# Moving the linear part of a fused attention and MLP kernel to another fill of its group

## The chip, the cores and the metric

The kernel runs on one core of one Trainium2 chip. The metric is device time of one execution in microseconds (us), as the median over several executions. Engines: PE is TensorE (matmuls), PEld its weight loads, DVE is VectorE, ACT is ScalarE, POOL is GpSimd, SP is SyncE.

## The reference

```python
# x: (4, 12480, 128), inducing: (32, 128), w_in: (128, 2048), w_out: (2048, 128)
def mab(q, kv):                      # softmax attention, scale 1/sqrt(128)
    s = scale * (q @ kv.transpose(0, 2, 1))
    a = softmax(s)
    return a @ kv
h = mab(I, x)                        # 32 inducing points read x
y = mab(x, h).reshape(-1, 128)       # each token reads the 32 points
z = y @ w_in
out = (max(z, 0) + alpha * min(z, 0)) @ w_out
```

The kernel never forms y. With e the unnormalised softmax of a token and hW = h @ w_in, it computes relu(e @ hW) @ ((1 - alpha) * w_out), plus a linear part e @ hA with hA = h @ (w_in @ (alpha * w_out)), and divides by the softmax sum at the end.

## The kernel before

Tokens are worked in groups of 512: 24 groups per batch, and one of 192 tokens (the remainder). A full group takes four *fills*, j = 0 to 3. A fill's four ring matmuls write one *ring bank* each, of six PSUM buffers used in turn; an *eviction* reads a bank with ReLU, and the bank is free for the next matmul when it ends. A *hold* here is time in which PE waits with its next matmul for another engine. The unit of time below is the *slot*: everything that PE executes from one fill's first matmul to that of the next.

```python
    def fill(st, g, j):
        ...
        for r in range(4):
            ps = bank()                       # next of the 6 PSUM ring banks
            for i in range(cp):
                mm(ps[:, i * t : (i + 1) * t],
                   st.hW[32 * r : 32 * r + 32, j * cp + i, :],
                   rep[32 * r : 32 * r + 32, :t])
            banks.append(ps)
        lin = j == 2 // cp and lin_groups(st.b, g)      # third fill
        if lin:
            linear(st, lin)
        bits, pos = plan[st.b * NG + g, j]
        for r, ps in enumerate(banks):
            if r == pos:
                flush()                       # finish of the group before
            if bits >> r & 1:                 # evict with ReLU on ACT ...
                pin(nc.scalar.activation(out=gt[:, r, :w], in_=ps[:, :w], func=RELU))
            else:                             # ... or on DVE
                pin(nc.vector.tensor_relu(gt[:, r, :w], ps[:, :w]))
        flush()
        return gt

    def lin_groups(b, g):                     # for even g: this group and the next
        if g % 2 == 0 and (b, g) != (0, 0):
            return [g, g + 1] if g + 1 < NS * NQ else [g]
        return []

    def linear(st, groups):                   # 8 small matmuls, two row groups side by side
        for k in range(NB):
            for r, g in enumerate(groups):
                ...
                    mm(accs[(st.b * NG + g) % 2][:pp, k, :],
                       st.rep[g][32 * r : 32 * r + 32, k * pp : (k + 1) * pp],
                       st.hA[32 * r : 32 * r + 32, :],
                       start=((r == 1 or cp > 1) and k == 0), stop=False, ...)

    def finish(st, g):                        # L446: DVE reads the accumulator, divides
        ...
        pin(nc.vector.tensor_tensor(out=ob[...], in0=acc[...], in1=rbc, op=MULT))
        ...                                   # L451: DMA of ob to out

    for b, g, j in fills:                     # the main loop
        gt = fill(states[b], g, j)
        for fn, _ in tasks.pop((b * NG + g, j), []):
            fn()                              # misc tasks of this slot
        if prev is not None:
            mm2(*prev)                        # 16 matmuls of the fill before, into acc
        prev = (states[b], g, j, gt)
```

There are two accumulators: even groups use one, odd groups the other. The linear part of an even group g also starts the accumulator of group g + 1, which is the one that group g - 1 used. That group's `finish` stands in fill (g, 1).

The misc tasks prepare the next batch and the next 2048 tokens: `a_scores` (first fill of odd groups), `a_accum` (accumulation over x, third fill of even groups), `b_scores` or `b_den` (last fill of even groups, in turn; `b_den` makes softmax denominators; `h_den`, once for each next batch, those of h, beside `b_scores`). Each takes a ring bank. `make_plan` is a search in the kernel that decides, from a cost model of the slots, which evictions go to ACT (`bits`) and where the finish stands (`pos`).

The softmax here doesn't subtract the row's maximum and nothing guards it: scores larger than these inputs give would overflow.

## Time and profile before

| | before |
|---|---|
| time, first measured | 617.91 us |
| a plain fill, start to start | 1.327 us |
| slot with the linear part alone, held / free | 1.840 / 1.543 us |
| eviction of 128x512 | ACT 0.60, DVE 0.69 us |
| finish of a full group (ob) on DVE | 0.68 us |

The page's first lines (engine: busy us, share of the span, instructions):

```profile
span 615.7 us, 21682 instructions
## 1 busy us (share of the span) xinstructions
PE 596.0 (97%) x9179; PEld 436.4 (71%) x9180; DVE 520.3 (84%) x899; ACT 507.6 (82%) x998; POOL 89.0 (14%) x151
```

PE sets the pace, but 97% doesn't say that it never stands still. The Trainium skill ("Perfetto Trace Analysis", section "Tensor Engine Instruction (MATMUL, LD_WEIGHTS)") says that the profiler computes a matmul's end from its size and a delay for SBUF. The trace agrees that the spans are no measure of throughput: the 16 matmuls of a fill into its accumulator use the whole array and start 0.056 us apart, yet each is drawn 0.22 us long. So starts are what to read.

The timeline of DVE and PE around the third fill of an even group (start us, length us, engine, line, operation, out<-in, shape, count):

```profile
273.65 0.69 DVE L397 TENSOR_SCALAR gt<-ring_85 128x512 bf16<-128x512 f32 x1
...
274.25 0.68 DVE L446 TENSOR_TENSOR ob<-acc_87,rd 128x512 f32<-128x512 f32 x1
274.46 0.38 PE L94 MATMUL ring_82<-rep,hW 32*128 32x512 bf16 x1
...
274.68 0.21 PE L94 MATMUL acc_88<-hA,rep 32*128 32x128 bf16 x1
...
274.99 0.21 PE L94 MATMUL acc_87<-hA,rep 32*128 32x128 bf16 x1
274.99 0.22 PE L94 MATMUL acc_88<-hA,rep 32*128 32x128 bf16 x1
275.04 0.21 PE L94 MATMUL acc_87<-hA,rep 32*128 32x128 bf16 x1
```

The linear part starts at 274.68 in the even accumulator, acc_88. Its second matmul, into acc_87, starts 0.31 us later. Between them nothing happens on PE but the end of modelled spans. The finish of the odd group before, which reads acc_87, ends at 274.25 + 0.68 = 274.93; the semaphore that ended the matmul's wait was updated at 274.95. This is hold 1.

The timeline of PE and ACT a little earlier, around the last fill of an even group and the first of the odd group:

```profile
240.37 0.39 PE L94 MATMUL ring_84<-rep,hW 32*128 32x512 bf16 x1
...
240.70 0.25 PE L94 MATMUL ring_82<-pick,e_4543 128*128 128x4 bf16 x4
240.81 1.05 PE L94 MATMUL acc_88<-W_169,gt 128*128 128x128 bf16 x16
...
241.34 0.59 ACT L395 ACTIVATE gt<-ring_85 128x512 bf16<-128x512 f32 x1
241.80 0.38 PE L94 MATMUL ring_83<-rep,hW 32*128 32x512 bf16 x1
241.80 0.39 PE L94 MATMUL ring_84<-rep,hW 32*128 32x512 bf16 x1
241.98 0.37 PE L94 MATMUL ring_85<-rep,hW 32*128 32x512 bf16 x1
241.99 0.38 PE L94 MATMUL ring_86<-rep,hW 32*128 32x512 bf16 x1
```

This last slot, with b_den, takes 241.80 - 240.37 = 1.43 us. In the odd group's first fill the third ring matmul starts 0.18 us after the second: it needs ring_85, which the second ACT eviction of the fill before gave free at 241.93. This is hold 2.

### The profile page before, as it was taken

Reading aid. Unit: us, or ns where it says so; the run is one execution under the profiler, and the core shown is the slowest. Engines: PE = TensorE matmul, PEld = TensorE weight load, DVE = VectorE, ACT = ScalarE, POOL = GpSimd, SP = SyncE. Lnnn points to the kernel's source line nnn. Section 1 sums busy time; section 2 is a strip of 40 time slices with the busy share of each in tenths; the row PEclk is TensorE's granted clock in tenths of the full one; section 3 lists DMA queues with packets and bytes.
Section 4 is the critical chain, followed back from the end, with each engine's and each line's share of the span. In section 5 each row is a group of like instructions: output and inputs, shape, how many; then the busy total and the mean of one; then the engine's idle time right before and its main releaser. Section 6 shows DMA issues by size and latency. Waiting matters only on the chain. (4 is left out here: it accounts for less than half of the span.)

```text
span 615.7 us, 21682 instructions
## 1 busy us (share of the span) xinstructions
PE 596.0 (97%) x9179; PEld 436.4 (71%) x9180; DVE 520.3 (84%) x899; ACT 507.6 (82%) x998; POOL 89.0 (14%) x151
## 2 busy tenths in 40 slices
PE   5899999999999999999999999999999999999995
PEld 4577776777777777777777777777777777777774
DVE  4588888888888888888989898888888888888884
ACT  3688888888888888888888888888888888888884
POOL 7142112010011111110111111100101110110010
PEclk9999999999999999999999999999999999999998
DMA  9824999742125689972123599986112231221211
GB/s 142 172 69 93 185 168 169 155 115 69 65 85 129 137 151 175 155 160 88 56 80 94 112 185 164 162 154 138 53 60 76 87 96 46 87 96 45 88 56 43
DMA packets 87457, 68.66 MB, mean 111 GB/s; under 512 B 53200, under 2 KB 80736, under 8 KB 87360
## 3 DMA queue, kind: packets, MB, share of 16 engines
q0 software_dynamic: 21456, 39.82, 27.7%
q1 hardware_dynamic: 65904, 27.45, 23.5%
q8 instruction: 72, 1.18, 0.9%
q14 instruction: 25, 0.20, 0.1%
HBM read 39.94 MB, written 28.62 MB: 111 GB/s over the span
## 5 line engine op out<-in xcount | busy, mean ns | idle before, releaser
L94 PEld LDWEIGHTS <-gt 128*128 128x128 bf16 x6272 | 352.5, 98 | 73.6 <-issue 67.7
L94 PE MATMUL acc_87<-W_169,gt 128*128 128x128 bf16 (+1 forms) x3136 | 208.9, 220 | 0.0
L94 PE MATMUL acc_88<-W_169,gt 128*128 128x128 bf16 (+1 forms) x3136 | 208.8, 220 | 0.0
L451 POOL DMA_DIRECT2D out_dram<-ob x99 | 53.6, 541 | 501.8 <-DVE ob L446 445.0
L395 ACT ACTIVATE gt<-ring_84 128x512 bf16<-128x512 f32 (+1 forms) x162 | 96.9, 598 | 18.2 <-ACT gt L395 14.6
L395 ACT ACTIVATE gt<-ring_82 128x512 bf16<-128x512 f32 (+1 forms) x159 | 95.4, 600 | 14.8 <-ACT gt L395 9.7
L94 PE MATMUL ring_83<-rep,hW 32*128 32x512 bf16 (+1 forms) x269 | 101.1, 379 | 0.0
L94 PE MATMUL ring_84<-rep,hW 32*128 32x512 bf16 (+1 forms) x270 | 101.1, 378 | 0.0
L94 PE MATMUL ring_86<-rep,hW 32*128 32x512 bf16 (+1 forms) x267 | 100.4, 379 | 0.0
L94 PE MATMUL ring_81<-rep,hW 32*128 32x512 bf16 (+1 forms) x265 | 99.6, 379 | 0.7 <-ACT gt L395 0.4
L395 ACT ACTIVATE gt<-ring_86 128x512 bf16<-128x512 f32 (+1 forms) x149 | 89.2, 599 | 13.3 <-ACT gt L395 8.8
L94 PE MATMUL ring_85<-rep,hW 32*128 32x512 bf16 (+1 forms) x266 | 99.5, 378 | 0.0
L94 PE MATMUL ring_82<-rep,hW 32*128 32x512 bf16 (+1 forms) x263 | 98.8, 379 | 0.0
L395 ACT ACTIVATE gt<-ring_81 128x512 bf16<-128x512 f32 (+1 forms) x143 | 85.7, 599 | 15.5 <-ACT gt L395 11.6
L395 ACT ACTIVATE gt<-ring_85 128x512 bf16<-128x512 f32 x147 | 88.2, 600 | 11.4 <-ACT gt L395 7.8
L395 ACT ACTIVATE gt<-ring_83 128x512 bf16<-128x512 f32 (+1 forms) x142 | 84.9, 598 | 11.6 <-ACT gt L395 6.5
L397 DVE TENSOR_SCALAR gt<-ring_83 128x512 bf16<-128x512 f32 (+1 forms) x122 | 83.5, 685 | 12.0 <-PE ring_84 L94 5.6
L397 DVE TENSOR_SCALAR gt<-ring_81 128x512 bf16<-128x512 f32 (+1 forms) x117 | 80.1, 685 | 12.4 <-PE ring_83 L94 3.8
L397 DVE TENSOR_SCALAR gt<-ring_86 128x512 bf16<-128x512 f32 x113 | 77.6, 687 | 13.3 <-PE ring_81 L94 8.2
L397 DVE TENSOR_SCALAR gt<-ring_85 128x512 bf16<-128x512 f32 (+1 forms) x113 | 77.1, 683 | 11.2 <-PE ring_81 L94 4.4
L397 DVE TENSOR_SCALAR gt<-ring_84 128x512 bf16<-128x512 f32 x102 | 70.1, 688 | 12.1 <-PE ring_85 L94 6.2
L397 DVE TENSOR_SCALAR gt<-ring_82 128x512 bf16<-128x512 f32 x99 | 68.0, 687 | 11.2 <-PE ring_83 L94 5.6
(330 smaller groups left out, 388.1 us busy)
## 6 DMA issues: line engine op xcount, KB each, us to landing
out_dram<-ob POOLq DMA_DIRECT2D x96, 256.0 KB, 2.7
rep<-e2d SPq DMA_DIRECT2D x92, 128.0 KB, 3.4
xn<-in_x_dram POOLq DMA_DIRECT2D x18, 512.0 KB, 6.3
xn<-in_x_dram POOLq DMA_DIRECT2D x12, 256.0 KB, 7.2
w_out_f<-in_moe_w_out_dram POOLq DMA_DIRECT2D x1, 1024.0 KB, 14.2
w_in_b<-in_moe_w_in_dram POOLq DMA_DIRECT2D x1, 512.0 KB, 12.2
xT<-xn SPq DMA_TRANSPOSE x18, 6.6
out_dram<-ob POOLq DMA_DIRECT2D x3, 96.0 KB, 2.0
```

The source lines that it names most:

```text
L94: return pin(nc.tensor.matmul(o, lhsT, rhs, start=start, stop=stop, **kw))
L395: pin(nc.scalar.activation(out=gt[:, r, :w], in_=ps[:, :w], func=RELU))
L397: pin(nc.vector.tensor_relu(gt[:, r, :w], ps[:, :w]))
L451: pin((nc.sync if last_one else nc.gpsimd).dma_start(out=out[t0 : t0 + pp * nb, :].rearrange("(p j) c -> p j c", j=nb), in_=ob[:pp, :nb, :],))
```

## The change

Its intent is to put the linear part into the last fill of the even group instead of the third, and to move the accumulation over x along with it. This is the whole diff; the search for the eviction plan runs anew on the moved costs.

```diff
-        lin = j == 2 // cp and lin_groups(st.b, g)
+        lin = j == NJ // cp - 1 and lin_groups(st.b, g)
...
-                at(k + 8, lambda n=n, u=u: a_accum(states[n], u), 2, (240, "D", 220))
+                at(k + 8, lambda n=n, u=u: a_accum(states[n], u), 3, (240, "D", 220))
...
-            lin = 240 if j == 2 // cp and lin_groups(b, g) else 0
+            lin = 240 if j == NJ // cp - 1 and lin_groups(b, g) else 0
```

## The prediction

> **What bounds the kernel now.** TensorE. On the page PE is busy 97% of 615.7 us, at a granted clock of 0.996; ACT 82% and DVE 84% evict PSUM with slack. In the timeline of PE a plain fill (4 ring matmuls, then 16 into an accumulator) repeats every 1.327 us; odd groups, finish included, run at that pace. Small holds hide in the 97%, because the modelled matmul spans overlap, so I read start-to-start times in the timeline.
>
> They show two holds.
> 1. The linear part. Its first matmul (even group's accumulator) starts 0.226 us after the fill's first. The second (odd group's accumulator) starts 0.30 us later in about 40 of 48 slots, 0.004 us later in the others: 0.05 us after the VectorE finish (ob, L446) of the previous odd group has ended reading that accumulator. That finish takes 0.68 us and stands behind an eviction. Held slots last 1.840 us, free ones 1.543 us (linear alone: 0.217 us). Later matmuls wait too: the Trainium skill, "TensorE: Matmul & The Clock Gate", Part 2, says that matmuls stay in program order and only weight loads are pulled ahead; the trace agrees, all later matmuls start after the held one. Sum: 12.0 us. The view of waits doesn't list it, as each gap between modelled spans is small.
> 2. Odd groups' first fills, after a short last slot of an even group (1.43 us, with the softmax denominators, b_den): third and fourth ring matmul wait 0.175 us for evictions. Sum: 5.4 us.
>
> **What the change does.** PE executes the same instructions. The linear part moves from the even group's third to its last fill, 1.33 us later; the accumulation over x (a_accum, 0.338 us of PE) moves along, so it still shares the linear's slot, now with b_scores (0.330 us) or b_den (0.100 us). The eviction plan is searched anew.
>
> - Hold 1 goes: the finish ends 0.25 us after the old linear start, so about 1.1 us before the new. Minus 12 us, all on the critical engine.
> - Hold 2 mostly goes: the even group's last slot grows from 1.43 to 1.64 us or more, so evictions are done before the next fill. Minus 2 to 4 us.
> - New holds: the last slot takes up to 6 ring banks at once, and 7 where a_accum, b_scores and h_den meet (three times), more than the ring's 6. Estimate: plus 0.5 to 2.5 us.
>
> ACT and DVE should give nothing back: odd groups already run plain fills with a finish without holds.
>
> **Predicted:** 604.0 us, range 601.5 to 608.0. Chances: faster by over 2% 0.70; within 2% 0.29; slower by over 2% 0.01. Hold 1 alone brings about 605.8, right at the 2% mark; hold 2 decides the side.
>
> **What would show it.** Right: the second linear matmul starts within 0.01 us of the first in all even groups; slots with linear and a_accum lose 0.30 us; ring matmuls of odd groups' first fills no longer split 2 and 2; plain fills stay at 1.327 us; ACT and DVE busy times unchanged. Wrong: linear still held, or third fills of even groups longer than 1.33 us, or a_scores slots longer.
>
> **What would make it wrong.** The new plan piles evictions on one engine; the bunched bank demand stalls the PE; the evictors used the held time to catch up, so that stalls reappear in following fills. Then the time lies at 606 to 611 us, within 2%.

## The result, and the profile after

| | before | after |
|---|---|---|
| median us (6 runs each) | 617.84 | 601.05 |
| lowest to highest us | 617.36 to 618.08 | 600.25 to 601.29 |

The ratio is 0.9728, 95% interval 0.9716 to 0.9741. The result is correct. The change is clearly faster by over 2%, and the time lies 0.45 us below the predicted range. Two repeats of the same kernel beside later experiments gave medians of 602.15 and 601.80 us, inside the range; the last experiment looks at why they differ. The miss of 0.45 us is thus smaller than the 1.1 us between two medians of the same kernel.

The page after:

```profile
span 599.0 us, 21695 instructions
## 1 busy us (share of the span) xinstructions
PE 581.7 (97%) x9180; PEld 434.7 (73%) x9180; DVE 521.2 (87%) x902; ACT 507.1 (85%) x995; POOL 89.2 (15%) x151
```

DVE and ACT do the same work (521.2 and 507.1 us) in a shorter span. PE is still "97% busy".

The timeline of PE and DVE after, in the last slot of the even group and the first of the odd group, with the finish of the odd group before:

```profile
232.41 0.68 DVE L446 TENSOR_TENSOR ob<-acc_87,rd 128x512 f32<-128x512 f32 x1
...
233.94 0.38 PE L94 MATMUL ring_83<-rep,hW 32*128 32x512 bf16 x1
...
234.17 0.21 PE L94 MATMUL acc_88<-hA,rep 32*128 32x128 bf16 x1
234.17 0.21 PE L94 MATMUL acc_87<-hA,rep 32*128 32x128 bf16 x1
...
234.49 0.25 PE L94 MATMUL ring_81<-pick,e_4540 128*128 128x4 bf16 x4
234.67 0.41 PE L94 MATMUL ring_82<-xn,e1T 128*32 128x128 bf16 x16
235.01 1.07 PE L94 MATMUL acc_88<-W_169,gt 128*128 128x128 bf16 x16
235.04 0.68 DVE L397 TENSOR_SCALAR gt<-ring_86 128x512 bf16<-128x512 f32 x1
...
236.01 0.39 PE L94 MATMUL ring_83<-rep,hW 32*128 32x512 bf16 x1
236.01 0.38 PE L94 MATMUL ring_84<-rep,hW 32*128 32x512 bf16 x1
236.02 0.39 PE L94 MATMUL ring_85<-rep,hW 32*128 32x512 bf16 x1
236.02 0.38 PE L94 MATMUL ring_86<-rep,hW 32*128 32x512 bf16 x1
```

The finish ends at 233.09, the linear pair starts together 1.08 us later (234.17), and the last slot is 2.07 us long. Its last eviction ends at 235.72, and the four ring matmuls of the odd group's first fill start together (236.01 and 236.02). Hold 1 is gone in all slots; hold 2 stays in 3 of the 48 first fills of odd groups (29 before).

To see where the time went I added up, from the trace's start times, all slots of one kind (remainder groups and the first four groups of the run apart). Sums in us of the traces; an E label is an experiment below:

| slots | before | after | E1 | E3 | E5 | E6 | E8 |
|---|---|---|---|---|---|---|---|
| even groups, third | 89.58 | 61.39 | 70.33 | 77.71 | 61.09 | 63.03 | 117.55 |
| even groups, last | 71.04 | 87.70 | 80.96 | 71.02 | 91.69 | 80.14 | 70.96 |
| odd groups, first | 72.67 | 68.03 | 68.03 | 72.74 | 68.05 | 78.24 | 72.55 |
| odd groups, third | 61.58 | 61.41 | 61.40 | 65.16 | 61.59 | 61.41 | 61.41 |
| odd groups, last | 62.02 | 62.01 | 62.02 | 62.02 | 62.02 | 62.34 | 73.84 |
| everything else | 258.86 | 258.47 | 258.12 | 258.73 | 258.23 | 258.27 | 260.80 |
| span | 615.75 | 599.01 | 600.86 | 607.38 | 602.67 | 603.43 | 657.11 |

From before to after, the third and last slots of even groups lose (89.58 + 71.04) - (61.39 + 87.70) = 11.53 us. The starts of the linear matmuls show 12.0 us of hold gone there, so new costs of about 0.5 us came in. The first slots of odd groups lose 4.64 us, all else 0.57 us.

### The profile page after: what moved, and what is told of

Same layout as the page of the kernel before. It is cut to its first block, busy times and chain, and to the rows that moved or that the text cites. A ratio compares the mean times of both kernels' runs of the same rounds, so it can differ in the third digit from the quotient of the medians.

```text
span 599.0 us, 21695 instructions
## 1 busy us (share of the span) xinstructions
PE 581.7 (97%) x9180; PEld 434.7 (73%) x9180; DVE 521.2 (87%) x902; ACT 507.1 (85%) x995; POOL 89.2 (15%) x151
## 4 chain that ended last, share of the span: by engine, by line
PE 94%; DMA 2%; POOL 2%; ACT 1%; issue 0%; DVE 0%; POOLq 0%
PE acc_88 L94 33%; PE acc_87 L94 33%; PE ring_82 L94 5%; PE ring_86 L94 5%; PE ring_84 L94 5%; PE ring_81 L94 4%; PE ring_83 L94 4%; PE ring_85 L94 4%; DMA xn<-in_x_dram 2%; POOL xn L125 1%; ACT gt L395 0%; POOL xnr L130 0%; PE ring_84 L156 0%; ACT rep L327 0%; ACT e1T L185 0%
## 5 line engine op out<-in xcount | busy, mean ns | idle before, releaser
L395 ACT ACTIVATE gt<-ring_81 128x512 bf16<-128x512 f32 x144 | 86.2, 599 | 13.6 <-ACT gt L395 6.4
L395 ACT ACTIVATE gt<-ring_83 128x512 bf16<-128x512 f32 (+1 forms) x143 | 85.5, 598 | 11.9 <-PE ring_86 L94 4.3
L397 DVE TENSOR_SCALAR gt<-ring_86 128x512 bf16<-128x512 f32 x115 | 79.0, 687 | 7.2 <-PE ring_82 L94 2.5
L397 DVE TENSOR_SCALAR gt<-ring_84 128x512 bf16<-128x512 f32 x104 | 71.5, 688 | 9.4 <-PE ring_86 L94 4.4
L397 DVE TENSOR_SCALAR gt<-ring_82 128x512 bf16<-128x512 f32 x101 | 69.4, 687 | 7.4 <-PE ring_84 L94 2.5
```

## The experiments

The main theory: the second linear matmul waited for the finish of the odd group before (hold 1), and a short last slot let evictions fall behind the next fill (hold 2). The rivals: the linear pair was slow for another reason; the moved accumulation or the new eviction plan brought the gain. All twelve runs gave correct results.

### E1: the linear part alone

```diff
-        lin = j == 2 // cp and lin_groups(st.b, g)
+        lin = j == NJ // cp - 1 and lin_groups(st.b, g)
-            lin = 240 if j == 2 // cp and lin_groups(b, g) else 0
+            lin = 240 if j == NJ // cp - 1 and lin_groups(b, g) else 0
```

> The linear part alone moves to the last fill of the even group; the accumulation over x stays in the third fill. Theory (the hold on the finish goes, and the longer last slot lets evictions finish): the 12.0 us of linear holds go and most of the 5.4 us of holds in odd groups' first fills too, since the last slot grows by 0.217 us: 601 to 603 us. Rival (the bunching of tasks or the move of the accumulation is needed for the rest): only the 12 us go, 605 to 606 us.

Measured: 603.18 us, ratio 0.9769 (0.9753 to 0.9785), a little above the expected 601 to 603. Both holds are gone: the linear pair starts together, and odd groups' first slots sum to 68.03 us as in the changed kernel. So the linear part alone brings most of the gain (14.3 of 16.8 us). The even third and last slots are 2.2 us longer than in the changed kernel (151.29 against 149.09): in 26 of the third fills the fourth ring matmul is held about 0.12 us. The trace shows what precedes 24 of these: there the search has put the finish ahead of all evictions of the fill before (it starts 0.10 us into that fill, elsewhere about 1.1 us). E3 shows that this delays the evictions and so the next fill. Why the search chose it is open.

### E2: the accumulation alone

```diff
-                at(k + 8, lambda n=n, u=u: a_accum(states[n], u), 2, (240, "D", 220))
+                at(k + 8, lambda n=n, u=u: a_accum(states[n], u), 3, (240, "D", 220))
```

> The accumulation over x alone moves to the last fill; the linear part stays. Theory: the linear holds stay at about 12 us; of the holds in odd groups' first fills only those after last slots that now have b_den and an accumulation go (9 of them, 1.6 us); 615.5 to 617 us. Rival (the move of the misc tasks carries a good part of the gain): 612 us or less.

Measured: 616.73 us, ratio 0.9987 (0.9972 to 1.0002). Hold 1 stays at 12.0 us. Of the 29 held first fills of odd groups 13 are free, where 9 had been expected; 12 of them follow a last slot that got an accumulation and so grew (9 with b_den, 3 with h_den). Three others are newly held, by 0.07 us. The move of the misc tasks is worth under 1 us by itself.

### E3: the finish ahead of all evictions of its fill

```diff
-                    for pos in (0, 2, 4) if ended else (4,):
+                    for pos in (0,) if ended else (4,):
```

> The kernel before, with the finish always ahead of the evictions of its fill on VectorE. Theory (the second linear matmul waits for the finish): it ends about 0.6 us earlier, the linear holds go without moving the linear part: about 606 us, plus up to 5 us if the delayed evictions then hold ring matmuls. Rival (the linear pair is slow for another reason, such as the two row groups or the arrival of rep): linear holds stay, 617 to 619 us.

Measured: 609.26 us, ratio 0.9866 (0.9851 to 0.9881), as the theory says. The timeline of DVE and PE around a third fill of an even group, linear part in its old place:

```profile
187.92 0.69 DVE L446 TENSOR_TENSOR ob<-acc,rd 128x512 f32<-128x512 f32 x1 [0.23 <-PE acc L94]
...
189.15 0.49 PE L94 MATMUL ring<-rep,hW 32*128 32x512 bf16 x4
189.37 0.39 PE L94 MATMUL acc<-hA,rep 32*128 32x128 bf16 x8
189.69 1.07 PE L94 MATMUL acc<-W,gt 128*128 128x128 bf16 x16
```

The finish starts 0.10 us into the fill before (that began at 187.82), and all eight linear matmuls fit in 0.39 us. This slot lasts 1.544 us; in the kernel before the same slot was held and lasted 1.840 us. Hold 1 is gone, without moving the linear part. The even third slots give 11.9 us. The odd third slots take back 3.6 us: the finish now delays the evictions of its fill, and the fourth ring matmul of the next fill is about 0.1 us late in some 40 odd groups. In even groups the same delay shows on the ring matmul but costs nothing, because the linear part wouldn't start before 0.226 us anyway. So the wait is on the finish, and the rival (row groups, arrival of rep) falls.

### E4: the finish behind all evictions of its fill

```diff
-                    for pos in (0, 2, 4) if ended else (4,):
+                    for pos in (4,):
```

> The kernel before, with the finish always behind the evictions of its fill on VectorE. Theory: the linear holds grow from 0.30 us to 0.5 to 0.9 us each wherever the finish had an earlier place, the time rises to 626 to 642 us. Rival (another reason than the finish): no change, 617 to 619 us.

Measured: 618.39 us, ratio 1.0015 (1.0000 to 1.0030). This is a miss, and it looks like the rival's result. But the edit did not do what it should: the trace shows the finish in the same place as before, behind one DVE eviction, since the search had put three of that fill's four evictions on ACT. The hold is unchanged (12.0 us). It tells nothing about the theory.

### E8: the finish behind two evictions on DVE

```diff
-                for bits in range(1, 15):
-                    for pos in (0, 2, 4) if ended else (4,):
+                for bits in ((3, 5, 6, 9, 10, 12) if ended else range(1, 15)):
+                    for pos in (4,):
```

> The kernel before, with exactly two evictions on VectorE ahead of the finish in its fill (the run with the finish last did not have this: the search had put only one eviction on VectorE there, so the finish stood where it stood before). Theory (the second linear matmul waits for the finish): the finish ends one eviction, about 0.6 us, later, the linear holds grow from 0.30 to about 0.9 us: 638 to 644 us. Rival (another reason): holds stay 0.30 us, 617 to 620 us.

Measured: 659.03 us, ratio 1.0666 (1.0648 to 1.0684). The timeline of DVE and PE around a held slot; its idle time is now long enough for the profile to name who ended it:

```profile
201.42 0.68 DVE L446 TENSOR_TENSOR ob<-acc,rd 128x512 f32<-128x512 f32 x1
...
202.15 0.38 PE L94 MATMUL acc<-hA,rep 32*128 32x128 bf16 x7 [0.69 <-DVE ob L446]
```

One eviction more ahead of the finish makes this slot 2.439 us, where it was 1.840 us in the kernel before. So the hold follows the finish in both directions. The time is 15 us above what was expected: the even third slots grew by 28.0 us (47 of them held, not 41), and odd groups' last slots by 11.8 us of new ring holds, which I had not foreseen.

### E5: the changed order with the eviction plan of the old one

```diff
-    def at(slot, fn, j=1, cost=None):
+    def at(slot, fn, j=1, cost=None, plan_j=None):
...
+        if cost:
+            plan_costs.setdefault((slot, j if plan_j is None else plan_j), []).append(cost)
...
-                at(k + 8, lambda n=n, u=u: a_accum(states[n], u), 3, (240, "D", 220))
+                at(k + 8, lambda n=n, u=u: a_accum(states[n], u), 3, (240, "D", 220), 2)
...
-            lin = 240 if j == NJ // cp - 1 and lin_groups(b, g) else 0
-            costs = [c for _, c in tasks.get((b * NG + g, j), []) if c]
+            lin = 240 if j == 2 // cp and lin_groups(b, g) else 0
+            costs = plan_costs.get((b * NG + g, j), [])
```

> The changed kernel with the assignment of evictions and the place of the finish searched for the old slots (as in the kernel before). Theory (the gain is the waits on PE, not the new assignment): 600.5 to 602.5 us. Rival (the new search brings the part of the gain that the prediction lacked, about 3 us): 603 us or more.

Measured: 604.69 us, ratio 0.9796 (0.9782 to 0.9811). The rival holds here. Both holds are gone, but the last slots of even groups sum to 91.69 us against 87.70 us. The timeline of ACT, DVE and PE around one of them:

```profile
232.88 3.74 ACT L395 ACTIVATE gt<-ring 128x512 bf16<-128x512 f32 x7 [0.24 <-ACT gt L395]
...
233.53 0.68 DVE L446 TENSOR_TENSOR ob<-acc,rd 128x512 f32<-128x512 f32 x1
...
235.06 0.79 PE L94 MATMUL ring<-rep,hW 32*128 32x512 bf16 x4
...
235.49 0.40 PE L94 MATMUL acc<-hA,rep 32*128 32x128 bf16 x8
```

The old plan gives ACT seven evictions almost without a pause from 232.88 us. It was made for a third slot lengthened by the linear part; now that slot is plain, ACT falls behind, and the fourth ring matmul of the last fill waits 0.42 us for it (the wait ended as an ACT eviction ended, 235.44 us). The four ring matmuls, drawn as 0.40 us elsewhere, are drawn as 0.79 us. In this trace 26 last fills of even groups are held, by 0.35 us on average. The cost is less than 26 times that, since the linear part wouldn't start before 0.226 us anyway: a held slot with b_den and the accumulation lasts 2.278 us against 2.067 us. The slots' bunching does make new holds, and the new search is what avoids them.

### E6: the linear part one fill later still

```diff
-    def lin_groups(b, g):
+    def lin_groups(b, g, j):
-        if g % 2 == 0 and (b, g) != (0, 0):
-            return [g, g + 1] if g + 1 < NS * NQ else [g]
+        if g == NS * NQ:
+            return [g] if j == 1 else []
+        if g % 2 == 1 and (b, g) != (0, 1) and j == 0:
+            return [g - 1, g]
...
```

The calls of `lin_groups`, in `fill` and in the search, change with it.

> The changed kernel with the linear part one fill later still, in the first fill of the odd group. Theory: linear holds stay gone, but the even group's last slot is short again where b_den stands without an accumulation, so holds of about 0.175 us come back in some 15 first fills of odd groups: 603 to 604.5 us. Rival (those holds went for another reason than the length of the last slot): 600.5 to 601.5 us.

Measured: 605.48 us, ratio 0.9806 (0.9791 to 0.9821), slower than the changed kernel and beyond the expected 603 to 604.5. Hold 1 stays gone. With the last slot short again, ring matmuls of odd groups' first fills are held in 19 groups (3 in the changed kernel), as the theory says. But most of these holds are about 0.10 us long and cost little here: the linear part, now in this fill, doesn't start before 0.226 us anyway, and a slot with the linear part alone lasts 1.543 us with such a hold or without.

Last slots of even groups and first of odd together are 158.38 us against 155.73 us, and nearly all of that lies in the last slots. Without their 46 linear parts of 0.217 us, the last slots of the changed kernel would sum to 77.7 us; here they sum to 80.14 us. In 19 of them b_den itself waits for a ring bank: mostly it starts 0.42 us into the slot, 0.05 us after ACT has evicted its bank, against 0.33 us in the kernel before. So evictions do fall behind a short last slot again, but the cost comes in another place than the theory said.

The rest of the loss, 1.6 us in third fills of even groups, is of the kind seen in E1 and E3: in 20 of the fills before them the finish stands ahead of the evictions.

### E7 and E9: the accumulation next to a_scores

In the changed kernel's trace the accumulation adds 0.224 us to a slot where it follows b_scores (2.097 against 1.873 us) and 0.421 us where it follows b_den (2.067 against 1.646 us). Both b_scores and the accumulation write 32-column tiles; b_den uses the whole array. The Trainium skill ("TensorEngine Tiling (Array Packing)", section "Key Properties") says that changing the tiling mode drains TensorE, and these two numbers agree. So does a third: alone, in the kernel before, the accumulation adds 0.337 us (2.177 against 1.840 us). Counted from the order of the matmuls, it brings no further change of tile shape behind b_scores, one when alone and two behind b_den: 0.224, 0.337 and 0.421 us. E7 puts the accumulation beside a_scores, which also writes 32-column tiles:

```diff
-                at(k + 8, lambda n=n, u=u: a_accum(states[n], u), 3, (240, "D", 220))
+                at(k + 9, lambda n=n, u=u: a_accum(states[n], u), 0, (240, "D", 220))
```

> The changed kernel with the accumulation over x in the first fill of the odd group, next to a_scores. In the changed kernel's trace it costs 0.224 us of PE after b_scores (which also has 32-column outputs) and 0.421 us after b_den. Theory (two neighbours of the same matmul shape share a change of the array's mode): four accumulations per batch cost 0.22 us each, 1 to 2 us less in all: 599 to 600 us. Rival (no sharing, or new holds for banks): 601 us or more.

Measured: 601.64 us (600.40 to 603.06), ratio 0.9738 (0.9721 to 0.9754). Inconclusive: the accumulation costs 0.223 us beside a_scores as expected, but in 3 slots a_scores waited for a transpose of x, up to 1.8 us. E9 issues these transposes one group earlier:

```diff
-                at(k + 3, lambda n=n, u=u: a_xpose(states[n], u))
+                at(k + 2, lambda n=n, u=u: a_xpose(states[n], u))
```

> The accumulation next to a_scores, as in the run with that name, but the transposes of x are issued one group (about 6 us) earlier, since there a_scores waited for them in 3 slots (1.8, 0.5 and 0.3 us longer). Theory: those waits go and the shared change of the array's mode shows: 598 to 600 us. Rival (the waits only move to another DMA, or the sharing is eaten by bank waits): 601 us or more.

> The changed kernel again on the same chip, as reference for the run beside it: 600 to 601.5 us.

Measured on one chip: E9 600.49 us (600.16 to 600.89), ratio 0.9717 (0.9703 to 0.9732); the changed kernel again 602.15 us (601.15 to 602.48), ratio 0.9741 (0.9727 to 0.9756). E9 lies between its two expectations, and the repeat above its own. The waits for transposes are gone in E9. That is most of its lead: its trace, 599.00 us, is as long as the first trace of the changed kernel (599.01 us), in which no a_scores waited. The shared mode is real per slot, but two accumulations per batch now stand alone at 0.336 us, third and first fills of even groups gained small ring holds, and three later slots of odd groups, with `h_transpose`, grew from 1.639 to 1.756 us.

### E10: only the earlier transposes

The edit is the one-line diff of E9 alone, on the changed kernel.

> The changed kernel, only with the transposes of x issued one group (about 6 us) earlier; the accumulation stays in the last fill. In a repeat of the changed kernel (602.15 us) one a_scores waited 1.2 us for such a transpose, in its first profile none did (601.05 us). Theory (what separates the two is those waits): 600 to 601.3 us, at or below the repeat beside it, with less spread. Rival (chip to chip difference): the same time as the repeat beside it.

> The changed kernel again, beside the run before it: 600.5 to 602.5 us.

Measured on one chip: E10 600.77 us (600.32 to 601.10), ratio 0.9727 (0.9714 to 0.9740); the changed kernel beside it 601.80 us (600.66 to 603.79), ratio 0.9745 (0.9727 to 0.9762). The view of PE's waits of that repeat, and below it of E10 (waiter <- what ended the wait: us in total, times, longest us):

```profile
PE ring L94 <- DMA xT<-xn: 1.4, 2, 0.9
PE ring L94 <- DVE e1T L187: 1.3, 4, 0.5
```

```profile
PE ring L156 <- DMA xn<-in_x_dram: 1.8, 4, 0.8
PE ring L94 <- DVE e1T L187: 1.0, 3, 0.5
```

The line with xT<-xn has no counterpart in E10. In both repeats the first slots of odd groups are longer than 68.03 us (69.33 and 69.60 us), and all other slot sums of the main stage agree within 0.02 us; in E10 it is 68.03 us. So in the traces the difference comes largely from a transpose that lands late in some executions. The intervals of the two ratios overlap, so the gain of about 1 us in the median is likely rather than certain.

## Why the prediction was right or wrong

The direction, the size class (over 2% faster, 0.70) and the main mechanism were right. The time was outside the range, by 0.45 us at first measurement: the predicted gain was 13.9 us, the measured 16.8 us. What failed are two terms of the sum: the credit for hold 2 was too small, and new holds, in net, did not come. Point by point:

- **Hold 1, "minus 12 us".** Right. The traces show 12.0 us before and none after. That the wait is on the finish is shown by E3 (finish earlier, hold gone) and E8 (finish later, hold longer), and by the semaphore that ended it.
- **Program order on PE** (the skill's "TensorE: Matmul & The Clock Gate", Part 2). The trace agrees: the third linear matmul goes to the free accumulator, yet starts at 274.99 with the held second.
- **Hold 2, "minus 2 to 4 us".** This term failed in size, the mechanism is right: the first slots of odd groups gave 4.64 us. The prediction had the full sum, 5.4 us, and then credited about half for no reason in the trace. E1 (all but 3 holds gone), E2 (13 gone) and E6 (19 there again) show that the length of the last slot is what does it; that they go in E5 too shows that it is not the new plan.
- **New holds, "plus 0.5 to 2.5 us".** This term failed too. In the even third and last slots about 0.5 us came in, at the low end; elsewhere 0.57 us went away, for which the prediction had no term. So the net was about zero. The prediction said that the plan is searched anew, but named this only as a risk, and took its estimate from counting ring banks per slot. E5 shows what the new search was worth: with the old plan the last slots alone cost 4.0 us more. The slot with 7 bank demands does have its hold: h_den starts 1.120 us into it, 0.05 us after ACT has evicted its bank (1.067). By estimate that is 0.1 to 0.2 us late (behind other accumulations the next matmul of the whole array starts 0.151 us after the last start; here it is 0.256 to 0.318 us). It happens three times, so about 0.4 us in all.
- **"Hold 1 alone brings about 605.8".** Moving the linear part can't test it: E1 shows that this also removes hold 2, as the last slot grows by 0.217 us. E3 removes hold 1 alone, and supports it: 609.26 us less the 3.6 us of its new holds is 605.7 us.
- **Costs of the accumulation, "0.338 us".** Wrong in the new slots, without consequence for the sum: 0.224 us after b_scores, 0.421 us after b_den.

So the terms summed to about 3 us too little gain: 1.6 us from hold 2 (4.64 against a middle of 3) and about 1.5 us from new holds (about zero in net against a middle of 1.5). Whether the measured time lay just outside or inside the range was partly luck: the repeats, with their late transposes, lay inside.

## What to carry to other kernels

Where PE is drawn as 97% busy, read the starts of matmuls, slot by slot: a hold of 0.3 us, repeated 40 times, was 2% of this kernel and stood in no list of waits. A matmul that begins an accumulator belongs well after the last reader of that accumulator, because all later matmuls queue behind it. When tasks move between slots, redo whatever balances the other engines for the slots: with the old assignment about a quarter of the gain was lost here (12.8 us instead of 16.8 us). Where such a search also places an instruction that another engine waits for (here the finish), check in the trace where it put it.

## What the Trainium skill lacked or had wrong

- "Perfetto Trace Analysis" recommends the share of weight loads (and the share of peak FLOPs, which wasn't worked out here) over that of matmuls. Here it rose from 71% to 73%, in step with the shorter span, while PE stayed at 97%; but neither share shows where 12.0 us of holds lie. A hint to compare start-to-start times of a repeated unit (1.327 us against 1.840 us) is missing.
- "TensorEngine Tiling (Array Packing)" says that a change of mode drains TensorE, but gives no cost. Here an accumulation in 32-column tiles costs 0.224 us behind another such task, 0.337 us alone and 0.421 us behind one that uses the whole array. With none, one and two further changes of tile shape, that is about 0.1 us for each: an estimate, as no run isolates the drain.
- Nothing that the runs showed contradicts the pages used.
